# Three edits to the first pass of a convolution and two-product kernel: taps one join later, one sum on another engine, weight copies at a later turn

## The chip, the cores and the metric

The kernel runs on one core of a Trainium2 chip. The metric is the device time of one execution in microseconds (us); lower is better. In the text TensorE is PE in the profile, VectorE is DVE, ScalarE is ACT, GpSimd is POOL and SyncE is SP. GpSimd and SyncE also issue the transfers (DMAs) here; a transfer that GpSimd issues can add to what stands at its destination (`accum_op=ALU.add`), and this text calls such a transfer an accumulate.

## What is computed

```python
# x (8, 4096, 192), weight (8 heads, 7 taps), w_in (192, 2048), w_out (2048, 192)
w = softmax(weight, axis=-1)                      # per head
x_pad = concatenate([zeros(8, 6, 192), x], axis=1)
out = einsum('hk,bskhg->bshg', w, windows_of_7(x_pad))   # 24 channels per head
h = out.reshape(32768, 192) @ w_in
g = h * (1.0 / (1.0 + exp(-1.702 * h)))
return g @ w_out
```

A causal convolution of seven taps along the sequence, a product to 2048 hidden columns, a gate, and a product back to 192. All in float32.

## The kernel before, in words

The 32768 rows are worked in 32 parts of 1024 rows (`N_BIG`, the loop variable `big`). Every part passes three stages: the convolution, the first product with the gate (`hidden`), and the second product (`second`). Both products are written as sums of fewer, larger products: sums of weight blocks and sums of data blocks are made first, TensorE multiplies the sums (L709 for the first product, L1202 for the second), and the results are added and subtracted again ("joins", L817) before the gate is applied on ScalarE (L826 and L833). Part 0 is worked in another way, in `first_step`, while the weights are still being made. The change lies in the first pass of `hidden`, that of part 1, from about 89 to 144 us of the span.

The order of `hidden` is written out by hand in the list `HIDDEN` (L737): products `mm`, copies out of PSUM, `join`s, `gelu`s, and marks such as `turn` and `tap`. What a mark does depends on the part. In part 1 each `join` from the second on also takes one piece of extra work from the list `beside` (L810 to L820). The pieces, made in `second_first` (L1082 to L1087), first sum blocks of `w_in` on VectorE and then call `middle_tap(j)`, seven times in all.

`middle_tap(k)` (L1092) makes one tap of the convolution for the middle block of channels (64 to 127) of part 2: ScalarE multiplies the shifted input by the tap's weight and writes a 128x512 tile into a home that is free just then. Tap 0 goes to the result itself, in `conv_t`; taps 1 to 6 go to the six entries of `MIDDLE` (L1090). The homes of tap 2 and of tap 6 are the same tile, `(11, 2)`, so tap 6 may be written only when tap 2 has been read. The seven tiles are summed as a tree, whose pairs stand in `middle_pairs` (L1103), the first of each pair receiving the sum. `middle_tree(n)` (L1105) issues the next n pairs as accumulates from GpSimd. Before, one pair follows tap 2, one follows tap 4, two follow tap 6, and the last two follow the third `turn` (L860).

At taps 5 and 6 `middle_tap` also does one addition on VectorE each (L1099): the last two sums of the convolution's other blocks of part 2.

`turn()` (L845) stands in `HIDDEN` three times. In part 1 the first turn calls `add_forms(3)` (L475): four of the weight sums ("forms") of the second product, each a copy on ScalarE (L480, or L478 with the sign changed) followed by an accumulate from GpSimd (L482). The third turn changes the sign of four forms on ScalarE (`end_forms`, L486), runs what had been held back for part 2, and issues the end of the tap tree.

After that tree GpSimd makes five sums of convolution blocks (`sum_of`, L437), and then the accumulates of the second product (L1178). Each engine works through its own instructions in order, and GpSimd's transfers are issued in order from its queue.

Of the kernel before, what the change touches and what calls it, by code (L numbers as in the profile page):

```python
# [11 lines left out]
ALU = mybir.AluOpType  # L12
# [3 lines left out]
def kernel(  # L16
# [29 lines left out]
    nc = tc.nc  # L46

    B, S, D = x.shape
    H, K = weight.shape
# [31 lines left out]
    vec, act = nc.vector, nc.scalar  # L81
# [56 lines left out]
    def spot(i):  # L138

        if i >= SPOTS:  # L140
            return block(*divmod(i - SPOTS, NG))
        flat = osbs[:, i * BLK : (i + 1) * BLK] if i < 2 else room[:, ROOMS[i - 2], :]
        return flat.rearrange("p (k t) -> p k t", k=NG)
# [55 lines left out]
    def own(big):  # L199
        return conv_t[:, big % 2 * NR : big % 2 * NR + NR, :]  # L200
# [156 lines left out]
    for c in range(NC):  # L357
        part = sel[:, c, :].rearrange("i (h q) -> i h q", h=2)
        for sign in (1, -1):
            nc.gpsimd.affine_select(  # L360
                out=part,
                in_=part,
# [82 lines left out]
    def sums_w_in(v, n0=0, n1=None):  # L445
        for item in SUMS_W[v][n0:n1]:
            add_up(lambda j: w_in_s[:, j, v * P : (v + 1) * P], *item)
# [27 lines left out]
    def add_forms(stage):  # L475
        for dst, src, *sign in COPY_O[stage]:
            if sign:
                act.mul(form(dst), form(src), -1.0)  # L478
            else:
                act.copy(form(dst), form(src))  # L480
        for dst, src in SUMS_O[stage]:
            nc.gpsimd.dma_start(out=form(dst), in_=form(src), accum_op=ALU.add)  # L482
# [60 lines left out]
    def conv_src(big, c, k, ns=slice(0, 2)):  # L543
        return xts[big][:, c, ns, Q - PAD + k : Q - PAD + k + T]
# [230 lines left out]
    def hidden(big, tiles, work):  # L775
# [61 lines left out]
        def next_turn():  # L837
            c = next(turns)
            if c == 0:
                need(f"done {big + 1}")  # L840
            transpose_x(big + 2, c)
            if c == NC - 1 and big + 3 < N_BIG:
                load_x(big + 3)

        def turn():  # L845
            seen.append(0)
            if big > 1:
                if big + 2 < N_BIG:
                    next_turn()
            elif len(seen) == 1:  # L850
                add_forms(3)
            elif len(seen) == NC:
                while beside:
                    beside.pop(0)()
                need("forms")
                held.clear()
                waiting.pop(0)()
                held.append(0)
                middle_tree(2)
                next_turn()  # L860

                def last_turn():
                    next_turn()
                    held.clear()
                    while waiting:
                        waiting.pop(0)()

                beside.extend([next_turn, last_turn])
# [41 lines left out]
        seen, seen_taps, seen_joins, waiting = [], [], [], []  # L910
        held = [0] if big == 1 else []
        def add(eng, what):
# [3 lines left out]

        do = dict(
            add=add, mm=mm, copy=copy, join=join, gelu=gelu, turn=turn, tap=tap, early=early, vl=vl, fetch=lambda: fetch(big + 1, tiles[NEXT[0]]) if more else None,
            over=when_more(over), ve=when_more(lambda i: sum_of(big + 1, SUMS_H[i])),
            vc=when_more(lambda b: cross_run(big + 1, b, b + 1)),  # L920
# [8 lines left out]
    def second_first(between, fetch, last_taps):  # L929
# [151 lines left out]
        n = len(SUMS_W[FETCH[0]])  # L1081
        for j in range(max(K, (n - 2) // 2)):  # L1082
            def more(j=j):
                sums_w_in(FETCH[0], 3 + 2 * j, 5 + 2 * j)
                if j < K:
                    middle_tap(j)
            beside.append(more)  # L1087

    after_copy, beside = [], []
# [2 lines left out]
    def middle_tap(k):  # L1092
        dst = own(2)[:, 2:4, :]
        s, h = MIDDLE[k - 1]
        home = spot(s)[:, h : h + 2, :] if k else dst
        act.mul(home, conv_src(2, 1, k), cw[:, 1, k : k + 1])
        if k in (5, 6):
            out, src = tree.pop(0)
            vec.tensor_add(out, out, src)  # L1099
            assert len(tree) == 6 - k  # L1100
        middle_tree({2: 1, 4: 1, 6: 2}.get(k, 0))

    middle_pairs = [(1, 2), (3, 4), (5, 6), (0, 1), (3, 5), (0, 3)]  # L1103

    def middle_tree(n):  # L1105
        for i, j in [middle_pairs.pop(0) for _ in range(n)]:
            out, src = (
                spot(MIDDLE[q - 1][0])[:, MIDDLE[q - 1][1] : MIDDLE[q - 1][1] + 2, :] if q else own(2)[:, 2:4, :]
                for q in (i, j)
            )  # L1110
            nc.gpsimd.dma_start(out=out, in_=src, accum_op=ALU.add)

    def blocks(t):
        return t.rearrange("p (j t) -> p j t", t=Q)
# [157 lines left out]
    def need(label):  # L1272
        for q in (todo, ready):
            while any(item[0] == label for item in q):
                q.pop(0)[2]()
# [226 lines left out]
```

## Time and profile before

| what | value |
|---|---|
| median of 3 runs | 2270.1 us (2269.73 to 2271.09) |
| the profiled execution | 2269.52 us |
| its span, first to last instruction | 2267.8 us |
| mean granted TensorE clock | 0.998 |
| TensorE busy, 89 to 144 us | 47.13 of 55.00 us |
| TensorE busy, 144 to 178 us | 33.54 of 34.00 us |
| accumulates (queue q0) over the span | 168.52 MB |

The first product of part 1 lies in the first of the two stretches, its second product in the second one. All later lines come from one profiled execution. A row of the timeline gives the start, the time from the first start to the last end, the engine, the line, the operation with its tiles, the count, and in brackets the idle time ahead of it with what ended that. A row of the chain of waits gives start and length of a piece of the chain that ended last. Starts are in us from the start of the span.

### The profile page before, as it was taken

What the parts mean: (1) busy time and instruction counts of PE and PEld (TensorE: products, weight loads), DVE (VectorE), ACT (ScalarE), POOL (GpSimd) and SP (SyncE); (2) the same over time, 40 slices, a digit from 0 to 9 for tenths busy, and PEclk for the clock granted to TensorE, in tenths of its full rate; (3) what the DMA queues carried; (4) which work ended last, traced back from release to release, by engine and by line L of the source; (5) the groups of instructions that cost most, each with busy time, mean ns of one, the idle gap of its engine ahead of it and who ended that gap; (6) DMA issues with size and microseconds to landing.
All of it is one profiled execution on the core that took longest, in us unless ns stands there. A gap on an engine that the chain in (4) does not pass through costs nothing.

```text
span 2267.8 us, 63911 instructions
## 1 busy us (share of the span) xinstructions
PE 2252.2 (99%) x25090; PEld 1360.1 (60%) x25090; DVE 2111.8 (93%) x3265; ACT 1716.0 (76%) x3342; POOL 985.5 (43%) x1011
## 2 busy tenths in 40 slices
PE   9989999999999999999999999999999999999999
PEld 5457656656556666566665566665666656666554
DVE  8989999999999999999999999999999999999998
ACT  8867777777877777777777777787777877777854
POOL 1444544444543445434445435454344454344510
PEclk9999999999999999999999999999999999999999
DMA  9986778767788667787676886677876768765743
GB/s 205 178 164 144 143 144 169 148 135 142 138 159 163 140 138 143 148 168 143 138 147 135 162 160 139 138 142 150 169 142 138 147 136 166 156 136 114 138 96 71
DMA packets 342571, 330.71 MB, mean 146 GB/s; under 512 B 131712, under 2 KB 280832, under 8 KB 342272
## 3 DMA queue, kind: packets, MB, share of 16 engines
q0 software_dynamic: 66928, 168.52, 42.2%
q1 hardware_dynamic: 273696, 157.72, 30.3%
q8 instruction: 199, 3.26, 0.6%
q14 instruction: 100, 0.82, 0.1%
q10 hardware_dynamic: 1648, 0.39, 0.1%
HBM read 53.15 MB, written 25.17 MB: 35 GB/s over the span
## 4 chain that ended last, share of the span: by engine, by line
PE 93%; DMA 3%; DVE 2%; issue 1%; ACT 1%; POOL 0%; POOLq 0%; DVEq 0%; ACTq 0%
PE slot L709 35%; PE slot L1202 28%; PE sums L1202 17%; PE sums L709 12%; DMA g<-g 2%; DMA w_form<-w_form 1%; DMA w_form<-w_out_s 0%; DMA osbs<-in_moe_w_out_dram 0%; PE slot L1290 0%; DVE slot L817 0%; DVE g L437 0%; POOL conv_t L600 0%; DVE xt L518 0%; DVE conv_t L553 0%; DVE room L437 0%
## 5 line engine op out<-in xcount | busy, mean ns | idle before, releaser
L709 PE MATMUL slot<-conv_t,w_in_s 64*128 64x512 f32 x3372 | 827.4, 593 | 7.6 <-ACT g L826 6.1
L1202 PE MATMUL slot<-g,w_form 128*32 128x256 f32 x5872 | 713.4, 379 | 0.0
L709 PEld LDWEIGHTS slot<-conv_t,w_in_s 64*128 64x128 f32 x3372 | 458.8, 187 | 284.2 <-issue 173.1
L437 DVE TENSOR_TENSOR g<-g 128x1024 f32<-128x1024 f32 x372 | 443.4, 1219 | 14.7 <-ACT g L833 7.5
L1202 PE MATMUL sums<-g,w_form 128*32 128x256 f32 x3800 | 422.0, 379 | 0.0
L1202 PEld LDWEIGHTS slot<-g,w_form 128*32 128x32 f32 x5872 | 363.7, 110 | 90.0
L826 ACT ACTIVATE g<-slot 128x512 f32<-128x512 f32 x494 | 265.4, 624 | 127.2 <-PE slot L709 126.8
L709 PE MATMUL sums<-conv_t,w_in_s 64*128 64x512 f32 x1284 | 349.1, 592 | 0.7 <-ACT osbs L802 0.3
L1202 PE MATMUL slot<-g,w_out_s 128*32 128x256 f32 x4080 | 321.3, 379 | 0.5 <-DVE room L435 0.3
L1178 POOL DMA_DIRECT2D g<-g x124 | 116.3, 938 | 451.8 <-PE slot L1202 311.8
L1227 ACT COPY room<-slot 32x256 f32<-32x256 f32 x434 | 159.0, 366 | 186.4 <-PE slot L1202 173.8
L570 ACT ACTIVATE g<-xt,cw 128x512 f32<-128x512 f32 x389 | 270.3, 719 | 4.4
L437 POOL TENSOR_TENSOR conv_t<-conv_t 128x256 f32<-128x256 f32 x209 | 193.0, 941 | 155.3 <-PE slot L709 90.4
L1202 PEld LDWEIGHTS sums<-g,w_form 128*32 128x32 f32 x3800 | 210.8, 110 | 69.7
L1202 PEld LDWEIGHTS slot<-g,w_out_s 128*32 128x32 f32 x4080 | 166.0, 110 | 126.7 <-ACT g L826 11.4
L915 POOL TENSOR_TENSOR conv_t<-conv_t,g 128x512 f32<-128x512 f32 x174 | 238.8, 1394 | 4.5
L709 PEld LDWEIGHTS sums<-conv_t,w_in_s 64*128 64x128 f32 x1284 | 174.6, 187 | 103.1 <-issue 54.6
L833 ACT ACTIVATE g<-g 128x1024 f32<-128x1024 f32 x155 | 170.5, 1100 | 0.0
L915 POOL TENSOR_TENSOR g<-g 128x512 f32<-128x512 f32 x87 | 110.9, 1274 | 121.9 <-ACT g L570 119.7
L1227 ACT COPY room<-sums 32x256 f32<-32x256 f32 x217 | 79.5, 366 | 103.3 <-PE sums L1202 91.2
L709 PE MATMUL slot<-g,w_in_s 64*128 64x512 f32 x556 | 149.6, 590 | 0.0
L826 ACT ACTIVATE g<-sums 128x512 f32<-128x512 f32 x188 | 103.9, 615 | 59.6 <-PE sums L709 58.8
(253 smaller groups left out, 3912.4 us busy)
## 6 DMA issues: line engine op xcount, KB each, us to landing
g<-g POOLq DMA_DIRECT2D x124, 512.0 KB, 6.4
conv_t<-conv_t SPq DMA_DIRECT2D x844, 64.0 KB, 2.0
xin<-in_x_dram SPq DMA_DIRECT2D x240, 180.0 KB, 6.3
out_dram<-osbs SPq DMA_DIRECT2D x186, 128.0 KB, 2.6
g<-g POOLq DMA_DIRECT2D x66, 256.0 KB, 6.6
g<-g SPq DMA_DIRECT2D x248, 64.0 KB, 3.8
g<-room POOLq DMA_DIRECT2D x31, 512.0 KB, 6.1
g<-osbs POOLq DMA_DIRECT2D x30, 512.0 KB, 6.6
```

The costliest lines, as they stand in the source:

```text
L437: eng.tensor_sub(v(dst), v(a), v(b))
L570: act.mul(home, conv_src(big, c, k), cw[:, c, k : k + 1])
L709: nc.tensor.matmul(slot[h], w_in_s[halves[h], a, v * P : (v + 1) * P], src, start=first, stop=True, skip_group_check=True,)
L826: act.activation(dst[:, :, h, :], ot(bank(src, h)), AF.Gelu_apprx_sigmoid, scale=float(sign))
L833: act.activation(dst.rearrange("p o h t -> p h o t"), src, AF.Gelu_apprx_sigmoid, scale=float(sign))
L915: (vec if eng == "v" else nc.gpsimd).tensor_add(dst, dst, home)
L1178: nc.gpsimd.dma_start(out=spot(dst), in_=spot(a), accum_op=ALU.add)
L1202: nc.tensor.matmul(dst, w, t, start=first, stop=last, skip_group_check=True)
L1227: act.copy(to, d)
```

## The change

Four edits. The first turn no longer makes the four weight sums of the second product; the second turn does. The middle block's taps move by one piece: the first of the pieces has no tap, and tap k stands where tap k+1 stood. The pair of taps 1 and 2 is added by VectorE, in the call for tap 3, in place of an accumulate after tap 2. The order of the other pairs follows: (0, 1) and (3, 4) after tap 4, (5, 6) after tap 6, and (3, 5) and (0, 3) after the third turn as before.

```diff
@@ turn, in hidden
-            elif len(seen) == 1:
+            elif len(seen) == 2:
                 add_forms(3)
@@ the pieces, in second_first
                 sums_w_in(FETCH[0], 3 + 2 * j, 5 + 2 * j)
-                if j < K:
-                    middle_tap(j)
+                if 0 < j <= K:
+                    middle_tap(j - 1)
@@ middle_tap
-        middle_tree({2: 1, 4: 1, 6: 2}.get(k, 0))
+        if k == 3:
+            middle_tree(1, vec)
+        middle_tree({4: 2, 6: 1}.get(k, 0))
 
-    middle_pairs = [(1, 2), (3, 4), (5, 6), (0, 1), (3, 5), (0, 3)]
+    middle_pairs = [(1, 2), (0, 1), (3, 4), (5, 6), (3, 5), (0, 3)]
 
-    def middle_tree(n):
+    def middle_tree(n, eng=None):
...
-            nc.gpsimd.dma_start(out=out, in_=src, accum_op=ALU.add)
+            if eng is None:
+                nc.gpsimd.dma_start(out=out, in_=src, accum_op=ALU.add)
+            else:
+                eng.tensor_add(out, out, src)
```

## The prediction

> **What bounds the kernel now.** I read the page's busy times first, then the table of windows around the change, then the timelines of the four engines there, then the chain of waits.
>
> ```profile
> PE 2252.2 (99%) x25090; PEld 1360.1 (60%) x25090; DVE 2111.8 (93%) x3265; ACT 1716.0 (76%) x3342; POOL 985.5 (43%) x1011
> ```
>
> TensorE is busy for 99% of the span, so only its few gaps are to be had, and a gap closed early is kept to the end if nothing behind it waits for something that did not move.
>
> ```profile
> core 0: us, PE busy (x) PEld busy (x) DVE busy (x) ACT busy (x) POOL busy (x), PEclk, DMA share, GB/s
> 120.00:125.00 5.00, 0.90 (x4) 0.07 (x1) 0.00 (x0) 1.14 (x2) 0.13 (x1) 0.83 0.90 151
> 125.00:130.00 5.00, 2.96 (x7) 2.56 (x9) 4.41 (x9) 5.00 (x10) 2.47 (x3) 0.50 0.62 105
> ```
>
> Between 120 and 125 us nothing computes while the transfers run at 0.90; then the clock is 0.50. TensorE's timeline shows the gap and a small one ahead of it:
>
> ```profile
> 117.57 2.04 PE L709 MATMUL slot<-conv_t,w_in_s 64*128 64x512 f32 x7 [0.60 <-ACT osbs L802]
> ...
> 119.82 1.08 PE L709 MATMUL sums<-conv_t,w_in_s 64*128 64x512 f32 x3
> 127.04 6.32 PE L709 MATMUL slot<-conv_t,w_in_s 64*128 64x512 f32 x20 [6.14 <-ACT g L826]
> ```
>
> It waits 6.14 us for ScalarE, whose timeline says why:
>
> ```profile
> 106.44 0.93 ACT L480 COPY w_form<-w_out_s 128x384 f32<-128x384 f32 x2
> 107.40 0.51 ACT L480 COPY w_out_s<-w_form 128x384 f32<-128x384 f32 x1
> 107.82 0.52 ACT L478 ACTIVATE w_out_s<-w_out_s 128x384 f32<-128x384 f32 x1
> ...
> 114.70 1.08 ACT L826 ACTIVATE g<-sums 128x512 f32<-128x512 f32 x2
> 116.94 1.07 ACT L802 COPY osbs<-slot 128x512 f32<-128x512 f32 x2 [1.15 <-DMA out_dram<-osbs]
> 123.86 0.72 ACT L1096 ACTIVATE g<-xt,cw 128x512 f32<-128x512 f32 x1 [5.85 <-DMA g<-g]
> 124.49 1.04 ACT L833 ACTIVATE g<-g 128x1024 f32<-128x1024 f32 x1
> 125.43 2.04 ACT L826 ACTIVATE g<-slot 128x512 f32<-128x512 f32 x4
> ...
> 131.53 1.77 ACT L486 ACTIVATE w_form<-w_form 128x384 f32<-128x384 f32 x4
> ```
>
> At 123.86 tap 6 (L1096) has stood 5.85 us behind a transfer g<-g: its home is that of tap 2, which the accumulate of the pair (1, 2) still reads. The gates that TensorE and VectorE need (L833, L826) are queued behind it. The chain of waits names the same accumulate, and what comes after:
>
> ```profile
> 115.58 8.20 DMA g<-g
> ...
> 138.84 1.15 DVE sums L817
> 140.03 1.12 PE sums L709 x2
> ...
> 144.00 2.07 PE sums L1202 x35
> ```
>
> From the gate at 124.49 to the last join at 138.84 the chain runs over VectorE, so **after the gap VectorE is the bound**, not TensorE, until the second product starts at 144.00. VectorE's own rows:
>
> ```profile
> 116.34 0.69 DVE L1099 TENSOR_TENSOR g<-g 128x512 f32<-128x512 f32 x1 [1.75 <-DMA g<-g]
> ...
> 118.68 0.68 DVE L1099 TENSOR_TENSOR conv_t<-conv_t,g 128x512 f32<-128x512 f32 x1
> 125.56 1.23 DVE L437 TENSOR_TENSOR g<-g 128x1024 f32<-128x1024 f32 x1 [6.20 <-ACT g L833]
> ...
> 137.61 1.23 DVE L437 TENSOR_TENSOR room<-g,osbs 128x1024 f32<-128x1024 f32 x1
> 138.76 2.35 DVE L817 TENSOR_TENSOR sums<-g,room 128x512 f32<-128x512 f32 x2
> ```
>
> **The change, part by part.**
>
> *The pair (1, 2) on VectorE.* It takes one 256 KB accumulate out of GpSimd's queue and puts one 128x512 addition on VectorE, 0.69 us by the row at 116.34. In the built order it stands before the joins that start at about 113 us; VectorE idles 1.75 us at 116.34 and 6.20 us at 125.56, so it costs nothing there. Without that cover it would cost 0.7. Tap 6 now waits for this addition alone, some 8 us before its turn comes: the 5.85 us are gone.
>
> *What ScalarE does then.* At 116.94 it waits for the stores of part 0's output, which were issued by SyncE and do not move. I keep that start: of ScalarE's work ahead of it, the change only reorders the four weight copies (0.93 + 0.51 + 0.52 = 1.96 us, now just behind the gate at 114.70) and takes tap 5 away, so ScalarE still arrives 1.15 us early or more. An earlier landing of the stores would bring up to 1.2 us, a later one costs its delay. Behind the copies at 116.94 (1.07) now stands tap 5 (0.72) and then the gate L833: 116.94 + 1.07 + 0.72 = 118.73, against 124.49. **That is 5.8 us** earlier. Tap 6 follows after the four gates of L826, where TensorE has what it needs: TensorE came 127.04 − 124.49 = 2.55 us after the gate, so now at 121.3, against an end of its earlier work at 119.82 + 1.08 = 120.9. The gap goes from 6.14 to about 0.4 us.
>
> *What is late next: VectorE.* Its run from 125.56 starts 5.8 us earlier, at 119.8. The second of the two L1099 additions, which stood at 118.68 under the wait, now stands inside that run, as the taps moved by one join: 0.68 us more. That leaves 5.1 us.
>
> *GpSimd's adds beside VectorE.* GpSimd's rows, and the mean of the join in the row at 138.76 over all parts:
>
> ```profile
> 116.12 2.93 POOL L1111 DMA_DIRECT2D room<-g  x1
> ...
> 128.71 0.86 POOL L1111 DMA_DIRECT2D room<-room  x1 [2.10 <-issue]
> 132.51 0.86 POOL L1111 DMA_DIRECT2D conv_t<-room  x1 [2.95 <-issue]
> 136.34 5.35 POOL L437 TENSOR_TENSOR conv_t<-conv_t 128x256 f32<-128x256 f32 x5 [2.97 <-DMA conv_t<-room]
> 149.64 0.87 POOL L1178 DMA_DIRECT2D g<-g  x1 [7.95 <-PE slot L1202]
> ```
> ```profile
> room<-g POOLq DMA_DIRECT2D x1, 256.0 KB, 8.9
> ```
> ```profile
> L817 DVE TENSOR_TENSOR sums<-g,room 128x512 f32<-128x512 f32 x32 | 21.7, 719 | 0.0
> ```
>
> The two joins at 138.76 took 2.35 us where the mean makes 2 x 0.719 = 1.44: 0.9 too long, beside GpSimd's five adds from 136.34 on. Where do these adds go? Four form accumulates (192 KB each), (0, 1) and (3, 4) now make up what was in GpSimd's queue before; the last one before was issued at 116.12 and landed 8.9 us later, at 125.0, and the bytes are the same, so the new last form lands at about 125 too. Pair (5, 6) follows tap 6 (start 118.73 + 1.04 + 2.04 = 121.8), stands behind the last form and lands at about 126.5 (the accumulate at 116.12 landed 1.2 behind that of 115.58), and (3, 5) and (0, 3) take 3.8 us each as before (128.71 to 132.51 to 136.34): the adds start at about 134.2, 2 us earlier. The two joins, 5.1 us earlier, lie at 133.7 to 135: about one of them escapes, +0.45. Ends: +0.9, if both escape; −1.7, if each of the five adds stretches one VectorE instruction by 0.45 (5 x 0.45 = 2.3, less the 0.9 paid already). I take +0.45, by the starts; the L437 row at 137.61 beside the same adds kept its 1.23 us, which speaks against the lower end.
>
> *The weight copies at the second turn.* The first turn's ScalarE time (1.96 us) goes into the wait ahead of 116.94; the small TensorE gaps that it feeds up to there close into the same wait, so I count nothing. The forms are next needed by the sign changes at 131.53 − 5.8 + 0.72 (tap 6, now between) = 126.45; the one that rewrites a form's source is the last of the four, 1.77 x 3/4 later, 127.8. They land at 125.0: 2.8 us of cover. The second product's use of them is later still. Ends: nothing, or the delay itself if they land after 127.8.
>
> *Sum:* 5.8 − 0.7 + 0.45 = 5.6 us. Against the profiled execution's 2269.5 that is 2263.9; the median of the runs shown lies 0.6 above that execution, so I give **2264.5**. The bounds (stores up to 1.2 early; adds +0.45 or −2.15 against what I took, the latter being rival 3) make 2262.8 to 2266.6.
>
> One rule of the Trainium skill bears on the slow stretch. The page "TensorE: Matmul & The Clock Gate", section "Part 1: The HAM clock gate (the "warmup" mystery)", says that an idle window of about 3.4 us halves the array's clock until a window of that length has been busy. The trace agrees: 0.50 after the gap of 6.14. By that rule the change would also give back the slow stretch, which is the first rival.
>
> **The rivals.**
>
> 1. *TensorE is the bound after the gap, not VectorE.* Then the gain is 127.04 − 121.3 = 5.7 plus half of the 2.96 us that were busy at clock 0.50, 1.5: 7.2, so 2262.9, or 2262 with the stores early. For it: the slow stretch is real. Against it: the chain runs over VectorE from 126 to 140. Chance 0.12.
>
> 2. *The forms land late, and the sign changes (L486) take over as the wait.* ScalarE's copy out of PSUM and gates for VectorE's next joins are queued behind them. Form by form behind two more 256 KB accumulates at the loaded rate (8.20 us for the one at 115.58), the last could land at 129.5 to 131.5, 1.7 to 3.7 us after it is needed: gain 3.9 to 1.9, so 2266.2 to 2268.2. Against it: equal bytes in that queue. Chance 0.13.
>
> 3. *GpSimd's adds stretch VectorE throughout.* They now lie beside VectorE's 128x1024 sums ahead of the second product, all with two inputs in SBUF: gain 5.1 − 1.7 = 3.4, so 2266.7. For it: the 2.35 us row. Against: 1.23 at 137.61. The Trainium skill's "SBUF — State Buffer", section "Who interferes with whom", has it as a rule: a VectorE instruction with two SBUF inputs and a GpSimd instruction that reads SBUF exclude each other for a whole instruction; the trace agrees in the one row and not in the other. Chance 0.12.
>
> 4. *Slower: the tap tree's end comes late and holds GpSimd's queue.* Three accumulates in series ((5, 6), (3, 5), (0, 3)) stand ahead of the five adds, and the second product's first accumulate (149.64 before, 7.95 us of slack) is queued behind these. I have the adds end at 139.6 and that accumulate due at 149.64 − 5.6 = 144.0. If each of the three took 8.9 us, as the loaded row did, instead of 3.8, the adds would end 15.3 us later, at 154.9, 10.9 too late, and with 5.6 gained the kernel would be 5.3 slower: 2275.4. It turns slower than before from (4.4 + 5.6) / 3 = 3.3 us more per accumulate, 7.1 each. For it: the next loads of the input now start near the third of them. Against: 8 us were seen only with six accumulates in the queue. Chance 0.05.
>
> That the change doesn't remove the wait has no chance to speak of: in the built order tap 6 waits for VectorE's addition and for no transfer.
>
> **How the numbers follow.** The forecast has 0.58, the rivals 0.12, 0.13, 0.12 and 0.05. A measurement of this kernel tells 0.2%, 4.5 us, from no change, so faster means below 2265.6. The forecast lies there but for the case that the stores land an us or more later (0.04 of its 0.58), rival 1 wholly: 0.66. Rivals 2 and 3 and that case are within 0.2%: 0.29. Rival 4 is 0.05. The range reaches from rival 1 with early stores, 2262.0, over rivals 2 and 3 to 2268.3; only rival 4 and worse cases of rival 2 are left out.
>
> **What would show it.** Right: tap 6 (L1096) starts without a wait on a transfer, near 121.8; no 5 us window has a clock near 0.50 after 100 us; TensorE's gap ahead of its next products is under 1 us; VectorE's 128x1024 subtraction starts near 119.8 and the second product near 138.4; everything after runs 5 to 6 us earlier up to the end. Wrong: a ScalarE idle time ended by a transfer w_out_s<-w_form ahead of the L486 row (rival 2); 128x1024 sums well over 1.23 us (rival 3); GpSimd's first L1178 without a wait for TensorE and later than 144 (rival 4); or TensorE gaps between 155 and 178 us, where the second product's accumulates fill the transfer engines and could give the gain back.

## The result, and the profile after

The changed kernel takes 2264.55 us in the median of 9 runs (2263.68 to 2265.73), against 2270.1 us for 9 runs of the kernel before beside it: a ratio of 0.9976, with a 95% interval of 0.9965 to 0.9986. That is 5.55 us less, where 5.6 were forecast. The interval goes from 0.14% to 0.35% faster, so it takes in the 0.2% that the prediction set as its line. The profiled execution took 2263.68 us, with a span of 2262.0 us. Lines below the edit have moved down by five: L1183 is L1178 of before, and L1207 is L1202. Inside the edit L1114 is L1111, and L1116 is the new addition.

The two profiles are compared first by stretches: from 115 us to the first instruction of the second product, and from there to the next part's first product. Of the kernel before (143.94 and 178.62):

```profile
115.00:143.94 28.94, 22.07 (x82) 12.36 (x78) 21.30 (x34) 17.39 (x34) 12.85 (x14) 0.88 0.78 142
143.94:178.62 34.68, 34.22 (x625) 19.97 (x625) 32.24 (x50) 24.74 (x52) 11.22 (x13) 1.00 0.97 187
```

The same two stretches of the changed kernel (137.76 and 173.41), and the two 5 us windows of the prediction; columns as there, the first number after the comma is TensorE's busy time, the third from the right the granted clock:

```profile
115.00:137.76 22.76, 20.98 (x81) 11.04 (x79) 20.82 (x37) 19.19 (x39) 11.16 (x12) 1.00 0.87 155
137.76:173.41 35.65, 34.43 (x625) 19.81 (x624) 33.74 (x50) 24.75 (x52) 14.68 (x16) 1.00 0.98 189
...
120.00:125.00 5.00, 4.81 (x21) 2.53 (x19) 4.97 (x11) 5.00 (x10) 1.01 (x2) 1.00 1.08 173
125.00:130.00 5.00, 3.90 (x18) 1.97 (x16) 4.97 (x10) 4.95 (x11) 0.86 (x1) 1.00 0.56 96
```

The first product's stretch is 28.94 − 22.76 = **6.18 us shorter**, and the clock there is 1.00 in place of 0.88. The second product's stretch is 35.65 − 34.68 = **0.97 us longer**. So 5.21 us have been gained when the next first product starts; the two spans differ by 5.8, and the 0.6 more lies after that, where the change touches nothing. TensorE's timeline of the changed kernel shows both stretches (a bracket holds the idle time ahead of a row and what ended it):

```profile
121.38 4.76 PE L709 MATMUL slot<-conv_t,w_in_s 64*128 64x512 f32 x19 [0.19 <-ACT g L826]
128.53 1.18 PE L709 MATMUL slot<-conv_t,w_in_s 64*128 64x512 f32 x3 [1.09 <-ACT g L802]
142.37 0.42 PE L1207 MATMUL slot<-g,w_out_s 128*32 128x256 f32 x3 [0.94 <-DVE g L437]
```

The gap of 6.14 us is one of 0.19. New are a gap of 1.09, ended by ScalarE's copy out of PSUM, and one of 0.94 inside the second product, ended by VectorE. ScalarE's timeline:

```profile
106.61 1.08 ACT L826 ACTIVATE g<-slot 128x512 f32<-128x512 f32 x2 [2.13 <-DMA g<-g]
...
108.79 1.07 ACT L802 COPY osbs<-sums 128x512 f32<-128x512 f32 x2 [0.48 <-DMA out_dram<-osbs]
...
115.44 0.93 ACT L480 COPY w_form<-w_out_s 128x384 f32<-128x384 f32 x2
...
117.24 1.05 ACT L802 COPY osbs<-slot 128x512 f32<-128x512 f32 x2
...
118.81 1.05 ACT L833 ACTIVATE g<-g 128x1024 f32<-128x1024 f32 x1
119.76 2.05 ACT L826 ACTIVATE g<-slot 128x512 f32<-128x512 f32 x4
121.67 0.75 ACT L1096 ACTIVATE g<-xt,cw 128x512 f32<-128x512 f32 x1
...
126.17 1.83 ACT L486 ACTIVATE w_form<-w_form 128x384 f32<-128x384 f32 x4
```

Tap 6 (121.67) and the sign changes (126.17) start with no bracket, that is without a wait. But neither has the copy at 117.24 one: in this execution ScalarE did not wait for the stores there. It was held earlier, 2.13 us at 106.61 by an accumulate and 0.48 us at 108.79 by an earlier store of part 0's output; from that copy up to 130 us it has work without a break, the weight copies included. The chain of waits passes over that store, which takes 7.10 us from 101.58 on. VectorE's timeline of the changed kernel:

```profile
113.43 0.68 DVE L1116 TENSOR_TENSOR g<-g 128x512 f32<-128x512 f32 x1
...
119.89 1.23 DVE L437 TENSOR_TENSOR g<-g 128x1024 f32<-128x1024 f32 x1 [1.84 <-ACT g L833]
...
133.65 1.29 DVE L817 TENSOR_TENSOR sums<-g,room 128x512 f32<-128x512 f32 x2
134.85 1.28 DVE L817 TENSOR_TENSOR g<-room,slot 128x512 f32<-128x512 f32 x2
136.04 1.25 DVE L437 TENSOR_TENSOR osbs<-g 128x1024 f32<-128x1024 f32 x1
137.22 1.74 DVE L435 TENSOR_TENSOR g<-g,osbs 128x1024 f32<-128x1024 f32 x1
138.89 1.76 DVE L437 TENSOR_TENSOR osbs<-osbs,g 128x1024 f32<-128x1024 f32 x1
140.57 6.42 DVE L437 TENSOR_TENSOR g<-g 128x1024 f32<-128x1024 f32 x5
```

The same 128x1024 sums in the kernel before:

```profile
143.36 1.21 DVE L435 TENSOR_TENSOR g<-g,osbs 128x1024 f32<-128x1024 f32 x1
144.49 1.21 DVE L437 TENSOR_TENSOR osbs<-osbs,g 128x1024 f32<-128x1024 f32 x1
145.63 5.88 DVE L437 TENSOR_TENSOR g<-g 128x1024 f32<-128x1024 f32 x5
```

And GpSimd's timeline of the changed kernel:

```profile
130.89 0.86 POOL L1114 DMA_DIRECT2D conv_t<-room  x1 [3.22 <-DMA room<-room]
134.31 6.92 POOL L437 TENSOR_TENSOR conv_t<-conv_t 128x256 f32<-128x256 f32 x5 [2.57 <-PE slot L709]
144.62 0.87 POOL L1183 DMA_DIRECT2D g<-g  x1 [3.38 <-DVE g L437]
```

GpSimd's five adds (134.31 to 141.23) begin only 0.66 us into the row of the two joins, and these take 1.29 us in place of 2.35. The adds lie beside the 128x1024 sums. The first of these kept its time (1.25 at 136.04), the next two went from 1.21 to about 1.75, and the group of five from 5.88 to 6.42: 0.53 + 0.55 + 0.54 = 1.6 us. The 0.94 us gap is TensorE waiting for one of them.

One more thing is seen in the chain of waits. Of the changed kernel:

```profile
156.70 10.02 DMA g<-g
166.84 0.43 DVE g L437
```

Of the kernel before:

```profile
161.72 10.21 DMA g<-g
172.05 0.43 DVE g L437
```

In both, the way from the second product's middle to the next first product leads over one 512 KB accumulate of GpSimd that takes 10 us. It starts 161.72 − 156.70 = 5.02 us earlier and lands (start plus length) 171.93 − 166.72 = 5.21 us earlier, and the next first product starts 178.62 − 173.41 = 5.21 earlier. Whatever the stretch ahead gains or loses, it counts by how far it moves the landing of this transfer. In nine of the profiles on record, those two and seven of the runs below, the chain of waits passes over it, and the next first product starts 6.7 us after it lands in each.

### The profile page after: what moved, and what is told of

It is laid out like the page before. It is cut to its first block, busy times and chain, and to the rows that moved or that the text cites. A ratio compares the mean times of both kernels' runs of the same rounds, so it can differ in the third digit from the quotient of the medians.

```text
span 2262.0 us, 63909 instructions
## 1 busy us (share of the span) xinstructions
PE 2249.6 (99%) x25090; PEld 1355.6 (60%) x25090; DVE 2112.2 (93%) x3266; ACT 1715.5 (76%) x3342; POOL 987.1 (44%) x1010
## 4 chain that ended last, share of the span: by engine, by line
PE 96%; DVE 1%; DMA 1%; ACT 1%; issue 0%; SPq 0%; POOL 0%; DVEq 0%; ACTq 0%; POOLq 0%
PE slot L709 37%; PE slot L1207 28%; PE sums L1207 17%; PE sums L709 13%; PE slot L987 1%; DMA xin<-in_x_dram 0%; DMA g<-g 0%; DVE g L437 0%; DMA out_dram<-osbs 0%; PE sums L992 0%; SPq L99 0%; PE slot L992 0%; ACT g L833 0%; DVE g L817 0%; DVE room L437 0%
## 5 line engine op out<-in xcount | busy, mean ns | idle before, releaser
L1207 PE MATMUL slot<-g,w_form 128*32 128x256 f32 x5872 | 713.6, 379 | 0.0
L1207 PE MATMUL sums<-g,w_form 128*32 128x256 f32 x3800 | 422.0, 379 | 0.0
L1207 PEld LDWEIGHTS slot<-g,w_form 128*32 128x32 f32 x5872 | 363.6, 110 | 90.0
L1207 PE MATMUL slot<-g,w_out_s 128*32 128x256 f32 x4080 | 321.3, 379 | 1.2 <-DVE g L437 0.9
L1183 POOL DMA_DIRECT2D g<-g x124 | 115.9, 935 | 449.1 <-PE slot L1207 278.7
L1207 PEld LDWEIGHTS sums<-g,w_form 128*32 128x32 f32 x3800 | 210.8, 110 | 69.7
L1207 PEld LDWEIGHTS slot<-g,w_out_s 128*32 128x32 f32 x4080 | 165.7, 110 | 128.1 <-ACT g L826 11.4
L833 ACT ACTIVATE g<-g 128x1024 f32<-128x1024 f32 x155 | 170.6, 1101 | 0.0
```

The source lines that it names most:

```text
L833: act.activation(dst.rearrange("p o h t -> p h o t"), src, AF.Gelu_apprx_sigmoid, scale=float(sign))
L1183: nc.gpsimd.dma_start(out=spot(dst), in_=spot(a), accum_op=ALU.add)
L1207: nc.tensor.matmul(dst, w, t, start=first, stop=last, skip_group_check=True)
```

## The experiments

Each kernel was timed in five rounds against the kernel before on the same chip. That kernel's median was 2270.48 us in the first group (the first four below), 2270.36 in the second (the next four) and 2270.25 in the third.

**Each edit alone.** First the addition on VectorE alone, with the new order of the pairs; the taps and the weight copies stay where they were.

```diff
-        middle_tree({2: 1, 4: 1, 6: 2}.get(k, 0))
+        if k == 3:
+            middle_tree(1, vec)
+        middle_tree({4: 2, 6: 1}.get(k, 0))
```

> Theory W (the whole gain is tap 6's wait behind the accumulate of the pair (1, 2)): VectorE's addition alone ends that wait. ScalarE comes from the copies at 116.9 to tap 6 and then to the gate L833 at about 118.7, as in the changed kernel, and VectorE's second L1099 addition stays ahead of its bound run, so 5.5 to 6.3 us are gained: 2263.8 to 2264.6. Rival Q (what counts is that the four form accumulates leave the front of GpSimd's queue): the forms still stand at the first turn, so at most a third of the gain is there, 2268 or more.

Measured: 2264.87 us, ratio 0.9979 (0.9970 to 0.9988). It has the whole gain alone, 5.6 us, which lies in the 5.5 to 6.3 that W gave (the time itself is 0.3 above W's numbers, which were reckoned from a slightly lower time of the kernel before), and Q falls. In its profile the second product starts at 136.54, 1.2 us ahead of the changed kernel's, but it has more stretched sums and two TensorE gaps. Of its VectorE timeline the sums, and of its TensorE timeline the gaps:

```profile
139.32 7.49 DVE L437 TENSOR_TENSOR g<-g 128x1024 f32<-128x1024 f32 x5
```
```profile
141.12 0.42 PE L1207 MATMUL slot<-g,w_out_s 128*32 128x256 f32 x3 [0.92 <-DVE g L437]
145.60 0.42 PE L1207 MATMUL slot<-g,w_out_s 128*32 128x256 f32 x3 [0.82 <-DVE g L437]
```

The 512 KB accumulate is issued at 156.48 there (156.70 in the changed kernel): a lead of 1.2 us has become 0.2. It takes 10.71 us in place of 10.02 and lands at 167.19, 0.5 us later than in the changed kernel.

The weight copies at the second turn alone:

```diff
-            elif len(seen) == 1:
+            elif len(seen) == 2:
                 add_forms(3)
```

> Theory W: the accumulate of the pair (1, 2) stays but is issued ahead of the four form accumulates (768 KB, about 3.6 us at 1.2 us per 256 KB in that queue), lands at about 120.2 instead of 123.8, and tap 6 waits about 2 us instead of 5.85: gain 3 to 4 us, 2266.1 to 2267.1. Rival Q: the whole gain, 2264.5.

Measured: 2265.96 us, ratio 0.9981 (0.9972 to 0.9990), 4.5 us less, a little more than the 3 to 4 that W gave and short of Q's 2264.5. This edit alone lets the pair's accumulate into GpSimd's queue ahead of the four weight sums, and tap 6 waits 1.22 us in place of 5.85 (ScalarE's timeline; TensorE's below it):

```profile
119.94 0.72 ACT L1096 ACTIVATE g<-xt,cw 128x512 f32<-128x512 f32 x1 [1.22 <-DMA g<-g]
```
```profile
123.11 6.31 PE L709 MATMUL slot<-conv_t,w_in_s 64*128 64x512 f32 x19 [1.50 <-ACT g L826]
```

The taps one join later alone:

```diff
-                if j < K:
-                    middle_tap(j)
+                if 0 < j <= K:
+                    middle_tap(j - 1)
```

> Theory W: the accumulate still lands at about 123.8, but tap 6 now stands behind the four gates of L826, so TensorE gets its banks at about 121.3 and only what is queued behind tap 6 (the copies into PSUM, 128x512) waits, about 2 us: gain 2.5 to 3.5, 2266.6 to 2267.6. Rival Q: the forms are where they were: no gain, 2269.5 or more.

Measured: 2266.24 us, ratio 0.9983 (0.9974 to 0.9992), 4.2 us less: a little more than W gave, and far from Q. Tap 6 still waits for the transfer, but now behind the gates that TensorE and VectorE need:

```profile
124.65 0.72 ACT L1096 ACTIVATE g<-xt,cw 128x512 f32<-128x512 f32 x1 [2.45 <-DMA g<-g]
```

The copies and the shift together, with the accumulate kept on GpSimd, are the two diffs above in one kernel.

> Theory W: the accumulate lands at about 120.2 and tap 6 is reached at about 121.8, so nothing waits and the gain is that of the whole change although VectorE adds no pair: 2264 to 2265. Rival V (VectorE's addition is what is needed, and the two moves are beside the point): 2267 or more. Rival Q: 2264.5 as well.

Measured: 2265.15 us, ratio 0.9977 (0.9968 to 0.9985), 5.3 us less, 0.15 above W's numbers and far from V's, so V falls; tap 6 starts without a wait at 121.80, and its second product starts at 137.89, close to the changed kernel's 137.76.

So 5.6, 4.5 and 4.2 us alone, 5.3 for two of them and 5.55 for all: the edits do not add. Each takes tap 6's wait out of the way of the gates in its own manner, and the first that does so has most of it. The intervals of all five overlap, and those of the kernels with 5.3 to 5.6 tell nothing apart.

**What sets the rest.** Two things were taken one by one: GpSimd's five adds beside VectorE's sums, and the 512 KB accumulate. First the changed kernel with the five adds left out.

```diff
-            over=when_more(over), ve=when_more(lambda i: sum_of(big + 1, SUMS_H[i])),
+            over=when_more(over), ve=when_more(lambda i: sum_of(big + 1, SUMS_H[i]) if big > 1 else None),
```

> The changed kernel with GpSimd's five sums of convolution blocks for part 2 left out (the only work left out). Theory P (GpSimd's sums and VectorE's sums with two inputs in SBUF hold each other up, and this costs the second product's start, since VectorE is the bound there): VectorE's 128x1024 sums go back from 1.75 to about 1.21 us each, VectorE gains the 1.6 us that its rows from 137.2 to 147 are too long, and the kernel comes to 2262.3 to 2263.5. Rival S (ScalarE's unbroken run from 110 to 131 us sets the end, the stretched sums are hidden): 2264.5 as the changed kernel.

Measured: 2264.18 us, ratio 0.9973 (0.9963 to 0.9983). The mechanism is shown: the group of five sums is back at 5.88 us, and TensorE has no gap ahead of 150 us. The time that was forecast from it is not there; it is nearer to S's 2264.5, but S's reason, ScalarE's run, is not what the profile shows. Of its table of windows, then the timelines of VectorE and TensorE:

```profile
138.00:150.00 12.00, 12.00 (x217) 7.05 (x220) 11.97 (x12) 7.76 (x17) 1.76 (x3) 1.00 0.94 188
...
170.00:175.00 5.00, 4.02 (x52) 1.84 (x45) 4.88 (x14) 2.90 (x6) 1.15 (x2) 1.00 0.99 193
```
```profile
166.77 0.42 DVE L437 TENSOR_TENSOR g<-conv_t 128x256 f32<-128x256 f32 x1 [1.51 <-DMA g<-g]
```
```profile
171.48 0.42 PE L1207 MATMUL slot<-g,w_out_s 128*32 128x256 f32 x3 [0.98 <-DVE room L435]
```

What was won ahead of 150 us is waited away at 166.77, behind the 512 KB accumulate, and TensorE pays it at 171.48. The accumulate is issued at 156.13, 0.57 us earlier than in the changed kernel, but takes 10.55 us and lands 0.04 us earlier. The next first product starts at 173.34, against 173.41.

The other way, each of the five adds made twice:

```diff
-            over=when_more(over), ve=when_more(lambda i: sum_of(big + 1, SUMS_H[i])),
+            over=when_more(over), ve=when_more(lambda i: [sum_of(big + 1, SUMS_H[i]) for _ in range(2 if big == 1 else 1)]),
```

> The changed kernel with each of the five GpSimd sums for part 2 made twice (the second time over the same result). Theory P: five more VectorE instructions stretched by about 0.5 us, or GpSimd's first accumulate of the second product (3.4 us of slack) late: 2266 to 2267.5. Rival S: 2264.5.

Measured: 2267.72 us, ratio 0.9991 (0.9982 to 0.9999): 3.2 us more than the changed kernel's 2264.55, a little beyond what P gave. TensorE's timeline has two gaps early in the second product now; VectorE's (third row) has a late wait:

```profile
142.98 0.42 PE L1207 MATMUL slot<-g,w_out_s 128*32 128x256 f32 x3 [1.34 <-DVE g L437]
147.98 0.42 PE L1207 MATMUL slot<-g,w_out_s 128*32 128x256 f32 x3 [1.34 <-DVE g L437]
...
166.29 0.42 DVE L435 TENSOR_TENSOR room<-slot,room 96x256 f32<-96x256 f32 x1 [3.46 <-DMA osbs<-room]
```

This profile is of the slowest of its 11 executions (2269.9 us). The ten adds end at 151.87, and GpSimd issues the second product's first accumulate only then, 7.2 us later than in the changed kernel; the wait at 166.29 is behind a transfer issued after it. Both causes that P named are there, the stretched sums and the late accumulates, and this run does not tell how much each costs.

Two kernels kept the adds but moved them, and the steps that were queued with them, into the second product, two at each mark: the changed kernel so edited, and the kernel with the addition alone so edited.

```diff
-                    while waiting:
-                        waiting.pop(0)()
+                    deferred.extend(waiting)
+                    waiting.clear()
...
-            tap=next_tap, piece=next_piece, late=late_pieces,
+            tap=tap_and_more, piece=next_piece, late=late_pieces,
```

> The changed kernel with the same five sums and their transfers spread over the second product (two steps at each of its first seven tap marks, from about 147 us on) instead of ahead of it. Theory P: VectorE's sums at the start of the second product run at 1.21 us and the ones beside the moved sums are stretched where VectorE has some 1 us of idle time; 2262.8 to 2264.3. Rival S: 2264.5 or, with the sums' results late for the next first product, more.

> VectorE's addition alone (taps and weight copies where they were before) with the five sums spread in the same way. Theory P: here VectorE lost 2.7 us to the sums and ScalarE is some 1 us ahead of the changed kernel, so this is the fastest of the four, 2262 to 2263.5. Rival S: 2264 to 2265.

Measured: 2266.06 us, ratio 0.9984 (0.9975 to 0.9993), and 2267.42 us, ratio 0.9986 (0.9977 to 0.9995). Both lie above their forecast, by 1.8 and 3.9 us; for the first, S had allowed for more than 2264.5 if the sums' results came late. The profile of the first is that of its slowest execution (2268.65 us). GpSimd issues the 512 KB accumulate there at 160.36, 3.66 us later than in the changed kernel, and yet VectorE's instruction behind it starts at 167.01, against 166.84. What TensorE waits for there is other transfers, 0.45 us at 174.11 and then 2.04 (TensorE's timeline, then the windows):

```profile
179.29 2.13 PE L709 MATMUL slot<-g,w_in_s 64*128 64x512 f32 x4 [2.04 <-DMA g<-g]
```
```profile
175.00:180.00 5.00, 2.96 (x12) 1.32 (x10) 2.16 (x4) 3.03 (x6) 4.92 (x4) 0.95 0.68 147
```

The adds' place between the first and the second product is the better one, stretched sums and all. In the second of the two the second product started at 139.04 in the profile, and not ahead of the changed kernel's as expected: the stores held ScalarE 0.93 us at 118.51.

The last group took away that accumulate: in part 1 alone, VectorE adds the 128x1024 tile. First together with the adds left out, then in the changed kernel, then in the kernel with the addition alone, and beside them the changed kernel once more.

```diff
-            sum=sum_g, acc=lambda d, a: sum_g(d, a, "acc"),
+            sum=sum_g, acc=lambda d, a: sum_g(d, d, "+", a) if (big, d) == (1, 18) else sum_g(d, a, "acc"),
```

> The changed kernel without GpSimd's five sums for part 2 (left out, as in the run without them), and with one accumulate of part 1's second product (the 512 KB one that GpSimd issued at 156.1) made as a 128x1024 addition on VectorE. Theory D: that accumulate, landing some 10 us after its issue, ends the wait of VectorE at 166.8 and gave back there what the missing sums had saved; without it the gain shows: 2262.8 to 2263.7, about 1 us under the run without the sums (2264.2). Rival B: VectorE is the bound there itself, and the 1.2 us of an addition more take the place of the wait: 2264.2 to 2265.4.

Measured: 2262.25 us, ratio 0.9966 (0.9954 to 0.9978). That is even under what D gave, and B falls for this kernel. TensorE has no idle time from 137 us to the next first product (windows), and VectorE's instruction of 166.77 starts without a wait (timeline):

```profile
137.00:171.89 34.89, 34.89 (x628) 20.10 (x626) 34.24 (x52) 25.67 (x54) 10.31 (x12) 1.00 1.01 195
```
```profile
165.04 0.41 DVE L437 TENSOR_TENSOR g<-conv_t 128x256 f32<-128x256 f32 x1
```

> The changed kernel with only that one accumulate made as a VectorE addition. Theory D: little is there to win, since VectorE waited 0.5 us and TensorE 0.3 us behind that transfer: 2263.8 to 2264.5, against 2264.5 of the changed kernel. Rival B: VectorE's addition costs its 1.2 us: 2265 to 2265.8.

> Only the addition on VectorE and the new order of the pairs (taps and weight copies where they were), with that one accumulate made as a VectorE addition. Its second product starts 1.2 us earlier than that of the changed kernel. Theory D: some of that is kept: 2263.5 to 2264.6, against 2264.9 without the edit. Rival B: 2265 to 2266.

> The changed kernel as it is, for comparison on the same chip with the other three: 2264.0 to 2265.2. Both theories agree.

Measured: 2265.23 us, ratio 0.9978 (0.9969 to 0.9986); 2264.31 us, ratio 0.9974 (0.9963 to 0.9985); and for the changed kernel again 2265.0 us, ratio 0.9977 (0.9968 to 0.9986). The first lies outside D's numbers and inside B's; against the changed kernel beside it, it is no different. Its windows show why little is won:

```profile
137.00:173.23 36.23, 35.58 (x631) 20.27 (x627) 35.76 (x52) 26.21 (x55) 13.47 (x14) 1.00 0.97 189
```

VectorE (third busy time) works 35.76 of the 36.23 us up to the next first product: without the wait for the transfer it is itself the limit, stretched sums and the added 1.2 us included, as B has it. The second lies inside D's numbers, 0.6 us under the same kernel with the accumulate in the first group, which the intervals do not tell apart. Its second product started at 138.81 in the profile, and not 1.2 us ahead of the changed kernel's: the stores held ScalarE 1.90 us at 118.14.

Put together, in us:

| | accumulate as a transfer | accumulate on VectorE |
|---|---|---|
| five adds made | 2264.55, again 2265.0 | 2265.23 |
| five adds left out | 2264.18 | 2262.25 |

Either one removed alone brings nothing that can be told; both removed bring 2.75 us against the changed kernel beside them, and the slowest execution without both (2262.86) is faster than the fastest of that kernel (2263.76). They are two limits of nearly the same height, one behind the other: the landing of the transfer, and VectorE's work with the sums that the adds stretch. The version without both leaves work out, so it is no kernel to use, and no version that does all the work beat the changed kernel by more than the intervals allow.

**The stores.** The second profile of the changed kernel was that of its slowest execution out of 11, 2266.81 us. ScalarE's timeline:

```profile
119.13 1.07 ACT L802 COPY osbs<-slot 128x512 f32<-128x512 f32 x2 [1.81 <-DMA out_dram<-osbs]
...
120.72 1.05 ACT L833 ACTIVATE g<-g 128x1024 f32<-128x1024 f32 x1
```

Here the stores did hold ScalarE, and longer than before. The gate stands 1.9 us later than in the first profile, TensorE waited 2.38 us for that copy, and the next first product came at 176.59 in place of 173.41. So 1.9 us at the gate have become 3.2 at the next first product. The same kernel thus has executions in which this copy waits for the stores and executions in which it does not; in the first profile a store held ScalarE too, but at the earlier copy at 108.79, and for 0.48 us.

## Why the prediction was right, step by step

*Tap 6's wait goes, the gate comes 5.8 us earlier.* Right in size: L833 at 118.81, forecast 118.73. **The reason given was wrong for the profiled execution.** The step said that the stores keep ScalarE's copy at 116.94 and that ScalarE arrives 1.15 us early; it arrived at 117.24 by its own work, set by the waits at 106.61 and 108.79, and the stores were there. That the two starts lie 0.3 us apart is luck. Of a later store the step said that it costs its delay; in the other profile it cost more, 3.2 us for 1.9.

*The weight copies cost nothing.* Not decided. In the profiled execution they lie on ScalarE's path, which has no break there, and in one profile the kernel with the addition alone, which has neither them nor the later taps there, starts its second product 1.2 us earlier. But the two other profiles with the same work up to that point start theirs at 138.81 and 139.04, after the changed kernel's 137.76; in both the stores held ScalarE, 1.90 and 0.93 us. What the copies cost was not measured by itself. The forms landed in time, so rival 2 falls.

*VectorE's second addition, 0.68.* Right: 0.69 us at 122.64, inside the run that starts at 119.89 (forecast 119.8).

*The adds beside VectorE, +0.45.* **This term was mis-sized, in both directions.** Both joins escaped, not one: 2.35 − 1.29 = 1.06, where the kept half was to cost. So 125.56 − 119.89 = 5.67, less 0.69, plus 1.06, makes 6.04 of the 6.18 us measured up to the second product; 0.14 is left without a term. In the second profile of the changed kernel one of the two was still stretched (1.82 us for both at 136.02), as the term had it, so this differs between executions. Then the adds stretched the sums by 1.6 us, which is rival 3's mechanism, and TensorE lost 0.94 there. The row of 1.23 us on which I rested ("which speaks against the lower end") was no evidence: the instruction from 137.61 to 138.84 lay beside adds that stretched the joins next to it, and three of the sums that came beside the same adds here were stretched. Rival 3 was right on what happens and wrong on the price: with the adds left out, nothing that can be told came back at the end. Its price was also added up wrongly: 2.3 less 0.9 is 1.4 and not 1.7, which makes its gain 3.7 and its time 2266.4.

*The end.* Forecast 5.6 and measured 5.55 agree closer than the terms do, and that is luck: 6.18 won and 0.97 lost make 5.21, and 0.6 between the two executions was not traced to an edit. The prediction took for granted that what is won ahead of the second product is kept to the end. It is kept only as far as the landing of the 512 KB accumulate moves, which was 5.21 us. Its last sentence named gaps between 155 and 178 us as a sign; they are 0.17 us at 166 and 0.1 between 170 and 175 here, and show fully only when the adds are gone.

What sets that landing was not tested. The transfer took 10.0 to 10.8 us in eight profiles, but 8.08 (start 161.06) with the addition alone and the adds moved, so an earlier issue is not an earlier landing by as much. The transfer engines' busy share is 1.05 to 1.08 in every 5 us of the changed kernel from 150 to 175 us, so they may be the limit there; no run shows it.

*The other rivals.* Rival 1 (TensorE as the bound, 7.2 us) falls: after the gap TensorE waited 1.09 us for ScalarE at 128.53, and ScalarE and VectorE were both busy for 4.95 to 5.00 of each 5 us. Rival 4 falls: the tree's three accumulates took 4.1, 4.1 and 3.4 us from issue to the next step, the adds ended at 141.23, and the first accumulate of the second product waited 3.38 us for VectorE, not for them.

## What to carry to other kernels

When one wait is removed by three edits at once, run each alone: here every one had 4.2 to 5.6 of the 5.55 us. Before counting a gain as kept, look in the chain of waits for the next long transfer behind the stretch; the gain is how much earlier that transfer lands, which can be less than how much earlier it is issued. And where a profile shows a suspect that brings nothing when it is removed, look for the second one of the same height, and remove both.

## What the runs showed of the hardware

GpSimd's adds and VectorE's sums, all with both inputs in SBUF, slow each other. VectorE's 128x1024 sum took 1.21 to 1.25 us and, beside the adds, 1.74 to 1.76 (but 1.25 for the first sum beside them); GpSimd's five adds took 5.35 us beside joins, 6.92 in the changed kernel and 8.17 in the kernel with the addition alone. The Trainium skill's "SBUF — State Buffer", section "Who interferes with whom", states that such a pair excludes each other for a whole instruction; the stretched sums agree with that in kind, and without the adds they were gone; a sum was longer by some 0.5 us, and how long the two exclude each other was not measured by itself.

The granted clock fell to 0.50 around idle times much shorter than the 6.14 us of before. In the second profile of the changed kernel TensorE idled 2.38 us up to 119.77; in the kernel with the copies alone 1.50 us up to 123.11. Their windows of 1 us read, one kernel to a fence:

```profile
121.00:122.00 1.00, 1.00 (x4) 0.79 (x3) 0.20 (x1) 1.00 (x2) 0.00 (x0) 0.50 1.15 186
```
```profile
126.00:127.00 1.00, 1.00 (x5) 0.59 (x4) 1.00 (x3) 1.00 (x3) 0.00 (x0) 0.50 1.06 182
```

Yet after 1.83 us of idle time in the kernel with the addition alone and the adds moved, the clock stayed at 1.00 (TensorE's timeline and the windows):

```profile
173.97 0.42 PE L1207 MATMUL slot<-g,w_out_s 128*32 128x256 f32 x3 [1.83 <-DVE room L435]
```
```profile
174.00:178.00 4.00, 4.00 (x42) 1.98 (x44) 3.88 (x11) 2.30 (x5) 1.66 (x2) 1.00 0.94 185
```

So the length of one idle time does not decide by itself, and what does is open. The rule of the Trainium skill that the prediction names ("TensorE: Matmul & The Clock Gate", "Part 1: The HAM clock gate (the "warmup" mystery)": an idle window of about 3.4 us) agrees with the 6.14 us in that the clock fell, though by windows of 1 us it fell about 2.4 us after TensorE's last instruction there (0.65 from 123 to 124 us); it does not agree with the drops after 1.50 and 2.38 us.
